# One row of the output weights moved to 32 partitions and six DMA engines, and the residual copied on chip, in a decode layer of attention and gated FFN

## The chip, the cores and the metric

The kernel runs on one core of one Trainium2 chip. The time is device microseconds of one execution. The profile is a record of one execution; its span, the time from first to last recorded instruction, is about 1.7 us shorter than the device time. Every execution also reports its span (to 0.1 us) and its mean granted TensorE clock, so spans can be compared even where only one execution has a full trace.

## The reference, cut to what matters

```python
xn = layernorm(A_x)                                  # 8 tokens, D = 512
# attention: 32 query heads, 8 kv heads, the last 1024 cached positions
q = xn @ wq
o = softmax(q @ k.T * Dh**-0.5) @ v
s = o.reshape(8, 4096) @ wo                          # wo is 4096 x 512, 4 MB
g = silu((gelu(xn @ w_gate) * (xn @ w_up)) @ w_down)
return A_x + s * g
```

Everything is bf16 and every weight and cache byte is used once. The 47.5 MB that must come in from memory set the pace: the packets of queue q1, 47.46 MB, take 95.0% of the span of the 16 DMA engines.

## The kernel before: the parts that matter

`wo` is loaded as 128 partitions of 32 rows each, in shrinking pieces so that little is left to compute after the last one lands. Two tiny loads bring the residual x into the layout of the result.

```python
NOR = Hq * Dh // P                                        # 32
wo_rows = A_wo.rearrange("(p j) d -> p (j d)", j=NOR)
# ...
        if g == NGR:
            parts = [(0, 16), (16, 24), (24, 28), (28, 30), (30, 31), (31, 32)]
            wo_t = [load_wo(*q) for q in parts[:2]]
            for t in range(2):
                nc.sync.dma_start(
                    out=x_res[64 * t : 64 * t + B, :], in_=x_flat[:, t * 256 : (t + 1) * 256]
                )
            wo_t += [load_wo(*q) for q in parts[2:]]
# ... score, soft, values of the last groups; then the FFN
    hT = ffn_up()            # contains regroup(), which makes og, the attention output by row
    ffn_down(hT)
    nc.vector.tensor_copy(out=x_b, in_=x_res)
    s_ps = ps_big.tile([P, 512], FP32, name="big")
    for q, (j0, j1) in enumerate(parts):
        for j in range(j0, j1):
            for t in range(2):
                c0 = (j - j0) * D + t * 256
                nc.tensor.matmul(
                    s_ps[64 * t : 64 * t + 64, 0:256],
                    og[:, j : j + 2, :].rearrange("p m b -> p (m b)"),
                    wo_t[q][:, c0 : c0 + 256],
                    start=(j == 0), stop=(j == NOR - 1),
                    tile_position=(0, 64 * t), skip_group_check=True,
                )
    nc.vector.tensor_tensor(out=tmp, in0=s_ps[:, 0:256], in1=g_sb, op=ALU.mult)
    nc.vector.tensor_tensor(out=out_sb, in0=tmp, in1=x_b, op=ALU.add)
    # ... two output DMAs
```

The softmax here doesn't subtract the row's maximum and nothing guards it: scores larger than these inputs give would overflow.

Of the kernel before, what the change touches and what calls it, by code (L numbers as in the profile page):

```python
# [9 lines left out]
ALU = mybir.AluOpType  # L10
AX = mybir.AxisListType
BF16 = mybir.dt.bfloat16
FP32 = mybir.dt.float32
# [3 lines left out]
def kernel(  # L17
# [13 lines left out]
    nc = tc.nc  # L31

    B, Sq, D = A_x.shape
# [11 lines left out]
    P = nc.NUM_PARTITIONS  # L45
# [12 lines left out]
    consts = ctx.enter_context(tc.tile_pool(name="consts", bufs=1))  # L58
    wide = ctx.enter_context(tc.tile_pool(name="wide", bufs=NWIDE))
    ring = ctx.enter_context(tc.tile_pool(name="ring", bufs=NSLOT))  # L60
    persist = ctx.enter_context(tc.tile_pool(name="persist", bufs=1))
# [8 lines left out]
    ps_a = ctx.enter_context(tc.tile_pool(name="ps_a", bufs=1, space=bass.MemoryType.PSUM))  # L70
# [5 lines left out]
    def slot():  # L76
        return ring.tile([P, SLOT], BF16, name="slot", align_bytes=512)
# [4 lines left out]
    x_flat = A_x.flatten_outer_dims()  # L82
    x_sb = persist.tile([B, D], BF16, name="x_sb")
    x_res = persist.tile([P, D // 2], BF16, name="x_res")
    nc.gpsimd.memset(x_res, 0.0)



    wq_rows = A_wq.rearrange("(p k) n -> p (k n)", k=NDC)

# [8 lines left out]
    def load_kv(cache, b, i):  # L99
        t = slot()  # L100
        nc.sync.dma_start(
            out=t,
            in_=cache[b, i * HN : (i + 1) * HN, win0:Sk, :].rearrange(
                "n (p r) d -> p n (r d)", r=NKR
            ),
        )
        return t

    def load_up(w):
        return load_wide(w.rearrange("(p k) n -> p (k n)", k=NDC), 0, NDC * F)  # L110

    def load_down():
        return load_wide(B_w_down.rearrange("(p j) d -> p (j d)", j=FR), 0, FR * D)

    NOR = Hq * Dh // P
    wo_rows = A_wo.rearrange("(p j) d -> p (j d)", j=NOR)

    def load_wo(j0, j1):

        if (j1 - j0) * D > SLOT:  # L120
            return load_wide(wo_rows, j0 * D, j1 * D)
        t = slot()
        nc.sync.dma_start(out=t[:, 0 : (j1 - j0) * D], in_=wo_rows[:, j0 * D : j1 * D])
        return t

    groups = [(b, i) for i in range(NHALF) for b in range(B)]
    NGR = len(groups)
    k_t, v_t = {}, {}
# [16 lines left out]
        out=ident,  # L145
        in_=ident,
# [6 lines left out]
    perm = consts.tile([P, P], BF16, name="perm")  # L153
    nc.gpsimd.tensor_copy(
        out=perm.rearrange("p (h q) -> p h q", q=P // 32),
        in_=ident.rearrange("p (q h) -> p h q", q=P // 32),
    )
    ident_f = consts.tile([P, P], FP32, name="ident_f")
    nc.vector.tensor_copy(out=ident_f, in_=ident)
    ones_f = consts.tile([P, P], FP32, name="ones_f")  # L160
# [5 lines left out]
        out=hot.rearrange("n r (m j) -> n r m j", m=HN),  # L166
        in_=hot.rearrange("n r (m j) -> n r m j", m=HN),
# [9 lines left out]
        out=far.rearrange("n (c m) -> n c m", m=HN),  # L177
        in_=far.rearrange("n (c m) -> n c m", m=HN),
# [9 lines left out]
        out=selq,  # L188
        in_=ident.rearrange("p (m q) -> p q m", q=QW),
        axis=AX.X,  # L190
        op=ALU.add,
# [3 lines left out]
        out=selr.rearrange("p r q -> p (r q)"),  # L195
        in_=ident.rearrange("p (u c) -> p c u", u=4),
        axis=AX.X,
        op=ALU.add,
# [12 lines left out]
        out=xhat[0:B, :],  # L211
        in0=x_sb,
# [19 lines left out]
    oT_all = persist.tile([P, B, Hq], BF16, name="oT_all")  # L232
    og = persist.tile([P, NOR + 1, 32], BF16, name="og")
    nc.vector.memset(og, 0.0)

    kT_t, p_t, pT_t, ss_t, o_t = {}, {}, {}, {}, {}

# [16 lines left out]
    def score(g):  # L254

        b, i = groups[g]
        sc = ps_sc.tile([P, 512], FP32, name="sc_ps")
        sc_t[g] = sc
        kT = kT_t[g].rearrange("w (r k e) -> w r k e", k=P, e=2)
        nc.tensor.matmul(  # L260
            sc,
            hot.rearrange("n r q -> n (r q)"),
            far,
            start=True,
            stop=False,
            skip_group_check=True,
        )
        for e in range(2):
            for t in range(4):
                nc.tensor.matmul(  # L270
                    sc[32 * t : 32 * t + 32, :],
                    q2_all[:, i, b, e, :, :, :].rearrange("w r n j -> w (r n j)"),
                    kT[:, :, 32 * t : 32 * t + 32, e],
                    start=False,
                    stop=(e == 1),
                    skip_group_check=True,
                    tile_position=(0, 32 * t),
                )

    def soft(g):  # L280
        p = p_pool.tile([P, 512], BF16, name="p")
        acc = small.tile([P, 1], FP32, name="acc")
        nc.scalar.activation(  # L283
            out=p, in_=sc_t[g], func=ACT.Exp, scale=inv_sqrt_dh, accum_out=acc
        )
        p_t[g] = p, acc

    def turn_p(g):
        p, acc = p_t[g]
        pT = pT_pool.tile([P, 512], BF16, name="pT")  # L290
        nc.vector.transpose(out=pT, in_=p)  # L291
        pT_t[g] = pT
        ss = small.tile([P, QW], FP32, name="ss")
        nc.vector.tensor_scalar(
            out=ss, in0=selq, scalar1=acc[:, 0:1], scalar2=None, op0=ALU.mult
        )
        ss_t[g] = ss
# [43 lines left out]
    def regroup():  # L341

        zt = ffn_sb.tile([P, B * Hq], BF16, name="zt")
        nc.vector.transpose(out=zt, in_=oT_all.rearrange("p b h -> p (b h)"))
        rg = ps_a.tile([P, B, 32], FP32, name="rg_ps", tag="a")
        nc.tensor.matmul(
            rg.rearrange("p b j -> p (b j)"),
            perm,
            zt,
            start=True,  # L350
            stop=True,
        )
        nc.vector.tensor_copy(
            out=og[:, 0:NOR, 0:B], in_=rg.rearrange("p b j -> p j b")
        )


    for t in range(4):
# [3 lines left out]
    for k in range(NDC):  # L362
        for i in range(NHALF):
            for j in range(HN):
# [5 lines left out]
                    start=(k == 0),  # L370
                    stop=(k == NDC - 1),
                    tile_position=(0, 32 * j),
                    skip_group_check=True,
                )
    q_sb = persist.tile([P, NHALF, rep, 2, 2, Dh // 2], BF16, name="q_sb")
    for i in range(NHALF):
        for rr in range(2):
            copy = nc.scalar.copy if rr else nc.vector.tensor_copy
            copy(  # L379
                out=q_sb[:, i, :, :, rr, :],  # L380
                in_=q_ps[i].rearrange("p (j w e) -> p j e w", j=rep, e=2),
            )
    for i in range(NHALF):
# [8 lines left out]
        for e in range(2):  # L392
            for rr in range(2):
                copy = nc.scalar.copy if rr else nc.vector.tensor_copy
                copy(  # L395
                    out=q2_all[64 * rr : 64 * rr + 64, i, :, e, rr, :, :].rearrange(
                        "p b n j -> p j n b"
                    ),
                    in_=qT_ps[64 * rr : 64 * rr + 64, :, e, :, 0:B],
# [41 lines left out]
        )  # L441
        return hT

    x_b = persist.tile([P, D // 2], BF16, name="x_b")
    g_sb = persist.tile([P, D // 2], FP32, name="g_sb")
    nc.vector.memset(g_sb, 0.0)

# [29 lines left out]
    for g in range(NGR + 1):  # L477
        if g < NGR:
            v_t[g] = load_kv(A_v_cache, *groups[g])
            if g + 2 < NGR:  # L480
                k_t[g + 2] = load_kv(A_k_cache, *groups[g + 2])
        if g == NGR - 1:
            wg_t = load_up(B_w_gate)
            wu_t = load_up(B_w_up)
            wd_t = load_down()
        if g == NGR:

            parts = [(0, 16), (16, 24), (24, 28), (28, 30), (30, 31), (31, 32)]
            wo_t = [load_wo(*q) for q in parts[:2]]
            for t in range(2):  # L490
                nc.sync.dma_start(
                    out=x_res[64 * t : 64 * t + B, :], in_=x_flat[:, t * 256 : (t + 1) * 256]
                )
            wo_t += [load_wo(*q) for q in parts[2:]]
        if g < NGR:
            score(g)
            soft(g)
        if g + 1 < NGR:
            turn_k(g + 1, 0)
        if g < NGR:  # L500
            turn_p(g)
        if g + 1 < NGR:
            turn_k(g + 1, 1)
        if g:
            values(g - 1)
        if g + 1 < NGR:
            turn_k(g + 1, 2)
            turn_k(g + 1, 3)
        if g:
            gather(g - 1)  # L510
# [1 line left out]
    hT = ffn_up()  # L512
    ffn_down(hT)

    nc.vector.tensor_copy(out=x_b, in_=x_res)


    s_ps = ps_big.tile([P, 512], FP32, name="big")
    for q, (j0, j1) in enumerate(parts):
        for j in range(j0, j1):  # L520
            for t in range(2):
                c0 = (j - j0) * D + t * 256
                nc.tensor.matmul(  # L523
                    s_ps[64 * t : 64 * t + 64, 0:256],
                    og[:, j : j + 2, :].rearrange("p m b -> p (m b)"),
                    wo_t[q][:, c0 : c0 + 256],
                    start=(j == 0),
                    stop=(j == NOR - 1),
                    tile_position=(0, 64 * t),
                    skip_group_check=True,  # L530
                )
    tmp = ffn_sb.tile([P, 256], BF16, name="tmp")
    out_sb = ffn_sb.tile([P, 256], BF16, name="out_sb")
    nc.vector.tensor_tensor(out=tmp, in0=s_ps[:, 0:256], in1=g_sb, op=ALU.mult)
    nc.vector.tensor_tensor(out=out_sb, in0=tmp, in1=x_b, op=ALU.add)
    out_flat = out.flatten_outer_dims()
    nc.sync.dma_start(out=out_flat[:, 0:256], in_=out_sb[0:B, :])
    nc.scalar.dma_start(out=out_flat[:, 256:512], in_=out_sb[64 : 64 + B, :])
# [30 lines left out]
```

## Time and profile before

| | before |
|---|---|
| time, median (6 runs) | 120.83 us (120.77 to 120.98) |
| span of the profiled run | 119.1 us |
| data moved by queue q1 | 47.46 MB |
| last landing of the last `wo` load | 115.60 us |
| end of the last matmul, start of `tmp` | 115.96, 115.98 us |

Lines of the page of before: the span, the busy time by engine, the clock and DMA rows (40 slices of the span, tenths), and two of the DMA queues.

```profile
span 119.1 us, 2281 instructions
PE 86.8 (73%) x929; PEld 62.1 (52%) x929; DVE 64.2 (54%) x149; ACT 40.4 (34%) x78; POOL 4.2 (4%) x10
...
PEclk9999999555799999999999999999999965555999
DMA  4999999999999999999999999999999999999940
...
q1 hardware_dynamic: 6240, 47.46, 95.0%
q8 instruction: 7, 0.11, 0.3%
```

The DMA row is 9 from slice 1 to slice 37 and the chain of waits is 57% DMA, so DMA bounds the kernel. The DMA row ends with a 4 and a 0: not every engine is busy to the end. Queue q8 is no data of the kernel: seven packets of instructions, 16 KB each.

The end of the chain of waits of before (start us, length us, what):

```profile
100.62 13.72 DMA slot<-in_A_wo_dram
114.34 0.04 issue
114.38 0.63 PE big L523 x8
115.01 0.00 issue
115.02 0.63 PE big L523 x6
...
115.98 0.44 DVE tmp L534
```

The windows view of before (a one-microsecond stretch; busy time and count of each engine; then granted clock, DMA share, GB/s):

```profile
109.00:110.00 1.00, 0.00 (x0) 0.00 (x0) 0.46 (x2) 0.37 (x1) 0.00 (x0) 0.71 0.90 377
...
111.00:112.00 1.00, 1.00 (x24) 1.00 (x20) 0.41 (x1) 0.00 (x0) 0.00 (x0) 1.00 1.02 419
...
114.00:115.00 1.00, 0.79 (x12) 0.43 (x8) 0.00 (x0) 0.00 (x0) 0.00 (x0) 1.00 0.50 181
115.00:116.00 1.00, 0.94 (x9) 0.43 (x7) 0.02 (x1) 0.00 (x0) 0.00 (x0) 1.00 0.06 22
```

The DMA share falls to a half between 114 and 115 us and to 0.06 in the microsecond after.

The trace file also records each landing, though no view of the profile lists them: a load's semaphore is raised several times, 16 times for a `wo` load on 128 partitions and 8 times for an `x_res` load on 8. Each increment is taken here as the landing of one DMA engine; that is the author's reading, as the trace numbers no engines. All landings below are read from there. For the last load of before (row 31, 16 engines, times in us):

```
113.90 113.95 114.00 114.07 114.08 114.13 | 114.32 114.58 114.85 | 115.24 115.29 115.37 115.39 115.53 115.58 115.60
```

Six engines are done 1.1 to 1.7 us before the seven late ones, though an even share of the load's 128 packets of 1 KB is eight for each (an estimate: packets divided by increments). The change tries to use that.

### The profile page before, as it was taken

Reading aid. Unit: us, or ns where it says so; the run is one execution under the profiler, and the core shown is the slowest. Engines: PE = TensorE matmul, PEld = TensorE weight load, DVE = VectorE, ACT = ScalarE, POOL = GpSimd, SP = SyncE. Lnnn points to the kernel's source line nnn. Section 1 sums busy time; section 2 is a strip of 40 time slices with the busy share of each in tenths; the row PEclk is TensorE's granted clock in tenths of the full one; section 3 lists DMA queues with packets and bytes.
Section 4 is the critical chain, followed back from the end, with each engine's and each line's share of the span. In section 5 each row is a group of like instructions: output and inputs, shape, how many; then the busy total and the mean of one; then the engine's idle time right before and its main releaser. Section 6 shows DMA issues by size and latency. Waiting matters only on the chain.

```text
span 119.1 us, 2281 instructions
## 1 busy us (share of the span) xinstructions
PE 86.8 (73%) x929; PEld 62.1 (52%) x929; DVE 64.2 (54%) x149; ACT 40.4 (34%) x78; POOL 4.2 (4%) x10
## 2 busy tenths in 40 slices
PE   0013946786999999999998797977979843546680
PEld 0003813563767777686775584755847630133650
DVE  5340644643666866876694664945748424622211
ACT  4000314792443562464354342453424403001100
POOL 7600000000000000000000000000000000000000
PEclk9999999555799999999999999999999965555999
DMA  4999999999999999999999999999999999999940
GB/s 88 432 396 440 418 426 432 418 432 424 418 432 432 432 402 435 429 418 426 429 426 421 429 424 421 429 426 424 429 424 442 426 424 448 420 440 402 405 165 3
DMA packets 6281, 47.61 MB, mean 400 GB/s; under 512 B 728, under 2 KB 1024, under 8 KB 1280
## 3 DMA queue, kind: packets, MB, share of 16 engines
q1 hardware_dynamic: 6240, 47.46, 95.0%
q8 instruction: 7, 0.11, 0.3%
q10 hardware_dynamic: 32, 0.01, 0.0%
q14 instruction: 2, 0.02, 0.0%
HBM read 47.46 MB, written 0.01 MB: 399 GB/s over the span
## 4 chain that ended last, share of the span: by engine, by line
DMA 57%; PE 24%; DVE 10%; ACT 2%; SPq 2%; issue 1%; DVEq 0%
DMA wide_slot<-in_B_w_gate_dram 18%; DMA slot<-in_A_v_cache_dram 16%; PE t_ps L244 12%; DMA slot<-in_A_wo_dram 12%; DMA wide_slot<-in_A_wq_dram 11%; DVE kT L250 8%; PE sc_ps L270 5%; PE o_ps L304 3%; PE big L411 1%; PE big L523 1%; DVE q_all L395 1%; ACT q_all L395 1%; PE big L366 1%; DVE q_sb L379 1%; ACT p L283 1%
## 5 line engine op out<-in xcount | busy, mean ns | idle before, releaser
L250 DVE COPY kT<-t_ps 128x1024 bf16<-128x1024 bf16 x48 | 31.8, 688 | 26.4 <-PE t_ps L244 24.5
L244 PE MATMUL t_ps<-ident_f,slot 128*128 128x128 f32 x256 | 38.5, 301 | 7.8 <-DMA slot<-in_A_k_cache_dram 7.8
L244 PEld LDWEIGHTS t_ps<-ident_f,slot 128*128 128x128 f32 x256 | 31.2, 154 | 18.0 <-issue 7.2
L250 ACT COPY kT<-t_ps 128x1024 bf16<-128x1024 bf16 x16 | 16.2, 1012 | 16.9 <-PE t_ps L244 16.5
L283 ACT ACTIVATE p<-sc_ps 128x512 bf16<-128x512 f32 x16 | 9.6, 597 | 28.4 <-PE sc_ps L270 28.4
L270 PE MATMUL sc_ps<-kT,q_all 128*32 128x512 bf16 x128 | 10.7, 405 | 3.9 <-ACT q_all L395 1.8
L291 DVE STREAM_TRANSPOSE pT<-p 128x512 bf16<-128x512 bf16 x16 | 11.2, 703 | 2.8 <-ACT p L283 2.8
L304 PE MATMUL o_ps<-slot,pT 128*32 128x256 bf16 x256 | 10.1, 278 | 0.0
L324 PE MATMUL a_ps<-selr,o_sb 128*128 128x16 f32 x64 | 9.6, 263 | 0.4 <-ACT o_sb L314 0.3
L324 PEld LDWEIGHTS a_ps<-selr,o_sb 128*128 128x128 f32 x64 | 8.4, 192 | 0.6 <-ACT o_sb L314 0.6
L270 PEld LDWEIGHTS <-q_all 128*32 128x32 bf16 x128 | 3.3, 95 | 7.9 <-issue 3.2
L304 PEld LDWEIGHTS <-pT 128*32 128x32 bf16 x256 | 5.5, 97 | 2.9 <-issue 2.5
L314 ACT COPY o_sb<-o_ps 128x256 f32<-128x256 f32 x16 | 6.0, 378 | 1.3 <-PE o_ps L304 1.3
L260 PE MATMUL sc_ps<-far,hot 4*128 4x512 bf16 x16 | 6.4, 398 | 0.0
L411 PE MATMUL big<-wide_slot,xT 128*32 128x448 bf16 x32 | 3.4, 571 | 3.8 <-DMA wide_slot<-in_B_w_up_dram 2.2
L523 PEld LDWEIGHTS <-og 128*64 128x64 bf16 x64 | 3.5, 109 | 3.7 <-DMA wide_slot<-in_A_wo_dram 2.1
L220 PE MATMUL t_ps<-ident,xhat 32*128 32x32 bf16 x4 | 0.3, 195 | 6.6 <-DVE xhat L210 6.6
L320 PEld LDWEIGHTS a_ps<-ss,ones_f 128*128 128x128 f32 x32 | 4.8, 191 | 0.5 <-DVE oT_all L334 0.3
L453 PE MATMUL big<-wide_slot,hT 128*32 128x256 bf16 x28 | 3.2, 417 | 2.6 <-DMA wide_slot<-in_B_w_down_dram 2.6
L320 PE MATMUL a_ps<-ss,ones_f 128*128 128x16 f32 x32 | 4.9, 229 | 0.0
L333 DVE RECIPROCAL rs<-a_ps 128x16 f32<-128x16 f32 x16 | 4.0, 249 | 1.3 <-PE a_ps L324 1.2
L453 PEld LDWEIGHTS <-hT 128*32 128x32 bf16 x28 | 2.2, 142 | 3.9 <-DVE hT L438 3.4
(64 smaller groups left out, 50.5 us busy)
## 6 DMA issues: line engine op xcount, KB each, us to landing
slot<-in_A_k_cache_dram SPq DMA_DIRECT2D x16, 1024.0 KB, 19.7
slot<-in_A_v_cache_dram SPq DMA_DIRECT2D x16, 1024.0 KB, 19.8
wide_slot<-in_A_wq_dram SPq DMA_DIRECT2D x2, 2048.0 KB, 13.7
wide_slot<-in_A_wo_dram SPq DMA_DIRECT2D x1, 2048.0 KB
wide_slot<-in_B_w_gate_dram SPq DMA_DIRECT2D x1, 1792.0 KB, 21.4
wide_slot<-in_B_w_up_dram SPq DMA_DIRECT2D x1, 1792.0 KB, 23.2
wide_slot<-in_B_w_down_dram SPq DMA_DIRECT2D x1, 1792.0 KB, 25.0
slot<-in_A_wo_dram SPq DMA_DIRECT2D x1, 1024.0 KB
```

The lines of the kernel that those rows point to most:

```text
L244: nc.tensor.transpose(kp[:, c * P : (c + 1) * P], kw[:, rp * P : (rp + 1) * P], ident_f)
L250: copy(out=kT_t[g][:, t * 8 * P : (t + 1) * 8 * P], in_=kp.bitcast(BF16))
L260: nc.tensor.matmul(sc, hot.rearrange("n r q -> n (r q)"), far, start=True, stop=False, skip_group_check=True,)
L270: nc.tensor.matmul(sc[32 * t : 32 * t + 32, :], q2_all[:, i, b, e, :, :, :].rearrange("w r n j -> w (r n j)"), kT[:, :, 32 * t : 32 * t + ...
L283: nc.scalar.activation(out=p, in_=sc_t[g], func=ACT.Exp, scale=inv_sqrt_dh, accum_out=acc)
L291: nc.vector.transpose(out=pT, in_=p)
L304: nc.tensor.matmul(o_ps[32 * u : 32 * u + 32, :], pT_t[g][:, m * 32 : (m + 1) * 32], v_t[g][:, m * 256 : (m + 1) * 256], start=(m < 4), st ...
L314: nc.scalar.copy(out=o_sb, in_=o_ps)
L320: nc.tensor.matmul(a_ps[:, 0, :], ones_f, ss_t[g], start=True, stop=True, skip_group_check=True)
L324: nc.tensor.matmul(a_ps[:, 1, :], o_t[g][:, r * Dh : (r + 1) * Dh], selr[:, r, :], start=(r == 0), stop=(r == 1), skip_group_check=True,)
L453: nc.tensor.matmul(f_ps[64 * t : 64 * t + 32, 0:256], hT[:, j, :], wd_t[:, c0 : c0 + 256], start=(j == 0), stop=(j == FR - 1), tile_positi ...
L523: nc.tensor.matmul(s_ps[64 * t : 64 * t + 64, 0:256], og[:, j : j + 2, :].rearrange("p m b -> p (m b)"), wo_t[q][:, c0 : c0 + 256], start= ...
```

## The change

Intent: take the last row of each partition (row 31) away from the late engines. Of its 128 pieces of 1 KB, 126 go out with an outer dimension of 6, so that six DMA engines carry 21 packets each and the others none; the attention output is regrouped to match by five small matmuls with a selection matrix. The piece is multiplied third, so its engines have time. The residual is copied on chip from the x that is there already.

```diff
+    NX, XR = 24, 5
+    def load_last():
+        last = A_wo.rearrange("(p j) d -> p j d", j=NOR)[:, NOR - 1, :]
+        six = last[0:126, :].rearrange("(e m) d -> e m d", m=21)
+        wx = slot()
+        nc.sync.dma_start(out=wx[0:NX, 0 : XR * D], in_=six[:, 0:20, :])
+        nc.sync.dma_start(out=wx[NX : NX + 6, 0:D], in_=six[:, 20, :])
+        nc.sync.dma_start(out=wx[NX + 6 : 32, 0:D], in_=last[126:128, :])
+        return wx
 ... selx, a 128 x 5 x 32 selection matrix, made by POOL from perm; in regroup():
+        rx = ps_a.tile([32, XR, B], FP32, name="rx_ps", tag="a")
+        for r in range(XR):
+            nc.tensor.matmul(rx[:, r, :], selx[:, r, :], zt...[:, :, NOR - 1], ...)
+        nc.vector.tensor_copy(out=ox[:, 0:XR, 0:B], in_=rx)
 ...
-            parts = [(0, 16), (16, 24), (24, 28), (28, 30), (30, 31), (31, 32)]
+            parts = [(0, 16), (16, 24), (24, 28), (28, 30), (30, 31)]
             wo_t = [load_wo(*q) for q in parts[:2]]
-            ... two loads of x_res
+            wx = load_last()
             wo_t += [load_wo(*q) for q in parts[2:]]
 ...
-    nc.vector.tensor_copy(out=x_b, in_=x_res)
+    for t in range(2):
+        nc.gpsimd.tensor_copy(out=x_res[64 * t : 64 * t + B, :], in_=x_sb[:, t * 256 : (t + 1) * 256])
 ...
     for q, (j0, j1) in enumerate(parts):
+        if q == 2:
+            for r in range(XR):
+                project(ox, wx, r, r * D, NX if r else 32)     # 2 matmuls each
         for j in range(j0, j1):
             project(og, wo_t[q], j, (j - j0) * D)
```

More of the change, by code (lines that the diff above doesn't have):

```diff
@@ L157 @@
     )
+    selx = consts.tile([P, XR, 32], BF16, name="selx")
+    nc.gpsimd.memset(selx, 0.0)
+    six = perm[:, 0:126].rearrange("p (e m) -> p e m", m=21)
+    for r in range(XR):
+        nc.gpsimd.tensor_copy(
+            out=selx[:, r, 0:NX].rearrange("p (e i) -> p e i", i=4),
+            in_=six[:, :, r:20:XR],
+        )
+    nc.gpsimd.tensor_copy(out=selx[:, 0, NX : NX + 6], in_=six[:, :, 20])
+    nc.gpsimd.tensor_copy(out=selx[:, 0, NX + 6 : 32], in_=perm[:, 126:128])
     ident_f = consts.tile([P, P], FP32, name="ident_f")
@@ L234 @@
     nc.vector.memset(og, 0.0)
+    ox = persist.tile([32, XR + 1, 32], BF16, name="ox")
+    nc.gpsimd.memset(ox, 0.0)
     kT_t, p_t, pT_t, ss_t, o_t = {}, {}, {}, {}, {}
@@ L355, in regroup @@
         )
+        rx = ps_a.tile([32, XR, B], FP32, name="rx_ps", tag="a")
+        for r in range(XR):
+            nc.tensor.matmul(
+                rx[:, r, :],
+                selx[:, r, :],
+                zt.rearrange("p (b j) -> p b j", b=B)[:, :, NOR - 1],
+                start=True,
+                stop=True,
+                skip_group_check=True,
+            )
+        nc.vector.tensor_copy(out=ox[:, 0:XR, 0:B], in_=rx)
     for t in range(4):
@@ L442, in ffn_up @@
         return hT
-    x_b = persist.tile([P, D // 2], BF16, name="x_b")
     g_sb = persist.tile([P, D // 2], FP32, name="g_sb")
@@ L486 @@
         if g == NGR:
-            parts = [(0, 16), (16, 24), (24, 28), (28, 30), (30, 31), (31, 32)]
+            parts = [(0, 16), (16, 24), (24, 28), (28, 30), (30, 31)]
             wo_t = [load_wo(*q) for q in parts[:2]]
-            for t in range(2):
-                nc.sync.dma_start(
-                    out=x_res[64 * t : 64 * t + B, :], in_=x_flat[:, t * 256 : (t + 1) * 256]
-                )
+            wx = load_last()
             wo_t += [load_wo(*q) for q in parts[2:]]
@@ L513, with project @@
     ffn_down(hT)
-    nc.vector.tensor_copy(out=x_b, in_=x_res)
+    for t in range(2):
+        nc.gpsimd.tensor_copy(
+            out=x_res[64 * t : 64 * t + B, :], in_=x_sb[:, t * 256 : (t + 1) * 256]
+        )
     s_ps = ps_big.tile([P, 512], FP32, name="big")
+    def project(o, w, j, c0, n=P):
+        for t in range(2):
+            nc.tensor.matmul(
+                s_ps[64 * t : 64 * t + 64, 0:256],
+                o[0:n, j : j + 2, :].rearrange("p m b -> p (m b)"),
+                w[0:n, c0 + t * 256 : c0 + (t + 1) * 256],
+                start=(j == 0 and o is og),
+                stop=(j == NOR - 2 and o is og),
+                tile_position=(0, 64 * t),
+                skip_group_check=True,
+            )
     for q, (j0, j1) in enumerate(parts):
+        if q == 2:
+            for r in range(XR):
+                project(ox, wx, r, r * D, NX if r else 32)
         for j in range(j0, j1):
-            for t in range(2):
-                c0 = (j - j0) * D + t * 256
-                nc.tensor.matmul(
-                    s_ps[64 * t : 64 * t + 64, 0:256],
-                    og[:, j : j + 2, :].rearrange("p m b -> p (m b)"),
-                    wo_t[q][:, c0 : c0 + 256],
-                    start=(j == 0),
-                    stop=(j == NOR - 1),
-                    tile_position=(0, 64 * t),
-                    skip_group_check=True,
-                )
+            project(og, wo_t[q], j, (j - j0) * D)
     tmp = ffn_sb.tile([P, 256], BF16, name="tmp")
@@ L534 @@
     nc.vector.tensor_tensor(out=tmp, in0=s_ps[:, 0:256], in1=g_sb, op=ALU.mult)
-    nc.vector.tensor_tensor(out=out_sb, in0=tmp, in1=x_b, op=ALU.add)
+    nc.vector.tensor_tensor(out=out_sb, in0=tmp, in1=x_res, op=ALU.add)
     out_flat = out.flatten_outer_dims()
```

## The prediction

Engine 0, 1, 2, ... are names, here and in all that follows: 0 and 1 are the engines of a load on two partitions, and each further number is the engine that a load on one partition more adds. That the six engines of the change are 0 to 5, and those of the x_res loads 0 to 7, was an assumption. The sum came to 114.85 - 0.39 + 0.85 = 115.31 us for the last landing, so 0.30 us off 120.83, or 120.53 us. In it, 0.33 us (8 packets) and 0.06 us (x_res) were estimates from the landings of before, and 0.85 us is 21 packets at about 0.04 us.

> **What bounds the kernel.** DMA. The page's DMA row is 9 in every slice from 1 to 37, at 400 to 448 GB/s; the chain of waits gives DMA 57%. In the windows view the DMA share stays 0.94 or more from 95 to 113 us, then falls to 0.91, 0.50 and 0.06 in the next three microseconds. So the sixteen DMA engines do not finish together. The trace's landing records show it: the sixteen increments of the last wo load (row 31) come at 113.90 to 114.13 us (six), 114.32, 114.58, 114.85, then 115.24 to 115.60 (seven). The page's part 3 lists seven 16 KB instruction packets (0.9 to 1.0 us each in the trace); landings that were within 0.6 us at 20 us fall apart after such packets, one engine at a time. I take the seven late engines to be the seven hit by them.
>
> After the last landing comes a serial tail: two matmuls (timeline: 115.64, 0.31 us), tmp 0.44, out_sb 0.29, output issue and landing, to 119.1.
>
> **What the change does.** Row 31 costs every engine 8 packets of 1 KB: the landings of the last two loads differ by 0.29 to 0.34 us on each engine, about 0.038 us per packet. The two x_res loads (512 B packets) cost eight engines about 0.06 us. Both leave the late engines. In their place 126 of the 128 rows go out with outer dimension 6. [...] the x_res loads on 8 partitions landed in 8 increments, the wo loads in 16. So engines 0 to 5 get 21 packets (two of them 22), about 0.85 us, in place of 0.33 + 0.06.
>
> Are 0 to 5 the early ones? The x_res landings (engines 0 to 7) come at 111.47, 111.52, 111.63, 111.71, 112.14, 112.39, 112.93, 113.27: six early or middling, two late. I believe that the six are 0 to 5. The slowest of them ended at 114.85; it should now end at 114.85 - 0.39 + 0.85 = 115.31. Late engines end at 115.30. A balance: last landing 115.3 in place of 115.6.
>
> PE: ten matmuls of wx take the place of two. Issue interval is about 0.053 us (8 in 0.63, 16 in 1.06), so ten cost 0.53. They stand after rows 16 to 23 (issued by 113.97), when wx is in (about 113.1), and end near 114.5; rows 24 to 27 land at about 114.34, so PE is 0.15 late there, catches up before rows 28 and 29 (115.0), and waits for row 30 at 115.3. Last matmul ends near 115.65, was 115.96.
>
> Off the critical path: about 2.5 us of POOL work near 2 us (q2_all ready near 7 us, needed at 18.6); five small matmuls and a copy after regroup (PE waits for w_up until 101.5 anyway); x copied on POOL early; x_b copy dropped.
>
> **Predicted:** 120.83 - 0.30 = 120.53 us; 8 in 10: 120.30 to 120.90. Faster by over 2%: 0.005; within: 0.985; slower by over 2%: 0.01.
>
> **Would show it right:** first wx load landing in 6 increments, row 30 landing last near 115.3 with its sixteen increments closer together, tmp starting 0.3 us earlier, PE idle before row 30. **Wrong:** PE the releaser without a DMA wait, or an early half that stays early.
>
> **What could break it:** engines 0 to 5 include a late one (then about 0.5 us slower), instruction packets falling on other engines or at other times, 1 KB reads at a 32 KB pitch slower on six engines.

## More of the kernel before

The clock row shows two stretches at half speed; the second one ends three to four slices from the end.

TensorE has its full clock from 109.6 us on, just before the projection, and follows the loads.

All executions here were classed as fast, except one of the version called `five`, which was slow and is left out, and the single unclassified executions of the two probes.

Ratios below are the mean time of one kernel's fast runs over that of the other's of the same rounds, so not quite the ratio of the medians that are quoted.

## The result, and the profile after

The changed kernel took 121.59 us (median of 6 runs, 121.32 to 121.96), before 120.83 in the same rounds: ratio 1.0064, 95% interval 1.0046 to 1.0081. It is 0.76 us slower, where 0.30 us faster was forecast (120.30 to 120.90 us, eight times in ten).

Lines of the page after that answer to those of before:

```profile
span 120.2 us, 2317 instructions
PE 89.6 (74%) x942; PEld 64.0 (53%) x942; DVE 64.0 (53%) x149; ACT 40.5 (34%) x78; POOL 6.5 (5%) x21
...
PEclk9999999855599999999999999999999975555587
DMA  4999999999999999999999999999999999999910
```

The end of its chain of waits:

```profile
98.21 12.27 DMA wide_slot<-in_A_wo_dram
110.48 0.04 issue
110.53 6.57 PE big L557 x69
117.09 0.02 issue
117.12 0.44 DVE tmp L575
```

Its windows view:

```profile
109.00:110.00 1.00, 0.00 (x0) 0.00 (x0) 0.59 (x2) 0.27 (x1) 0.00 (x0) 0.50 0.90 377
...
111.00:112.00 1.00, 1.00 (x12) 0.84 (x10) 0.28 (x1) 0.00 (x0) 0.00 (x0) 0.50 1.05 422
...
114.00:115.00 1.00, 1.00 (x12) 0.83 (x10) 0.00 (x0) 0.00 (x0) 0.00 (x0) 0.50 0.48 176
115.00:116.00 1.00, 1.00 (x20) 0.71 (x14) 0.00 (x0) 0.00 (x0) 0.00 (x0) 0.98 0.03 10
```

Two things differ. First, the whole projection is one stretch of 6.57 us in which PE waits for nothing: its clock stayed at a half until 115.05 us, so it did 12 matmuls in a microsecond where before did 24, and it ended 1.1 us later than before's. Second, the landings. Of the first wx load (six engines), and of the last load (row 30, sixteen):

```
wx:      112.08 112.17 112.23 112.68 113.06 113.62
row 30:  113.57 113.67 113.74 113.79 | 114.34 114.50 114.51 114.80 114.87 115.03 115.05 115.09 115.10 115.14 | 115.34 115.84
```

One of the six engines lands its share 1.5 us behind the first, and ends the whole load at 115.84 us, 0.24 us after before's last landing. The engines that carry no wx end at 115.14 at the latest, by the spacing of the landings (wx to row 30 is 2.2 us on the latest engine, so 113.06 belongs to 115.34 and 113.62 to 115.84). So two theories stand:

- A, imbalance: one of engines 0 to 5 is a late one, and the 21 packets lengthen the latest path.
- B, clock: in this execution PE, with eight more matmuls in the projection and half a clock, finished last.

The slowdown is not a fluke of the profiled execution: the other five were also slower, 121.32 to 121.73 us, at a mean clock of 0.9, the same as before's. That mean does not decide between A and B, since it does not say where in the span the half clock fell: the profiled executions of onerow_five and extra_pe below also have 0.9, with half clock until 114.3 and 114.2 us, where before's ended at 109.6.

### The profile page after: what moved, and what is told of

Read it like the earlier page. It is cut to its first block, busy times and chain, and to the rows that moved or that the text cites. A ratio compares the mean times of both kernels' runs of the same rounds, so it can differ in the third digit from the quotient of the medians.

```text
span 120.2 us, 2317 instructions
## 1 busy us (share of the span) xinstructions
PE 89.6 (74%) x942; PEld 64.0 (53%) x942; DVE 64.0 (53%) x149; ACT 40.5 (34%) x78; POOL 6.5 (5%) x21
## 4 chain that ended last, share of the span: by engine, by line
DMA 52%; PE 30%; DVE 10%; ACT 4%; issue 1%; SPq 0%; DVEq 0%
DMA wide_slot<-in_B_w_gate_dram 18%; DMA slot<-in_A_v_cache_dram 16%; PE t_ps L269 13%; DMA wide_slot<-in_A_wo_dram 10%; DMA slot<-in_A_k_cache_dram 8%; DVE kT L275 6%; PE big L557 5%; PE sc_ps L295 4%; PE o_ps L329 3%; ACT q_all L431 2%; PE big L402 2%; DVE q_all L431 2%; ACT L308 1%; PE big L447 1%; DVE q_sb L415 1%
## 5 line engine op out<-in xcount | busy, mean ns | idle before, releaser
L269 PE MATMUL t_ps<-ident_f,slot 128*128 128x128 f32 x256 | 39.0, 302 | 6.8 <-DMA slot<-in_A_k_cache_dram 6.5
L557 PEld LDWEIGHTS <-og 128*64 128x64 bf16 x62 | 4.7, 156 | 3.1 <-DMA wide_slot<-in_A_wo_dram 2.1
L447 PE MATMUL big<-wide_slot,xT 128*32 128x448 bf16 x32 | 2.7, 467 | 3.7 <-DMA wide_slot<-in_B_w_up_dram 2.1
L557 PE MATMUL big<-wide_slot,og 128*64 128x256 bf16 x32 | 3.6, 421 | 1.7 <-DMA wide_slot<-in_A_wo_dram 1.7
```

Source lines behind the costliest of these rows:

```text
L269: nc.tensor.transpose(kp[:, c * P : (c + 1) * P], kw[:, rp * P : (rp + 1) * P], ident_f)
L557: nc.tensor.matmul(s_ps[64 * t : 64 * t + 64, 0:256], o[0:n, j : j + 2, :].rearrange("p m b -> p (m b)"), w[0:n, c0 + t * 256 : c0 + (t + ...
```

## The experiments

Each was run beside executions of before on the same chip (together they are one job); the table collects them. "Filling" means extra matmuls on unused data that keep TensorE's clock up (mean clock 0.943 to 0.971 in the executions of warm_before, 0.886 to 0.927 in those of before beside them). "Span" is the median over the executions, "over before" its distance to before's median span of the same job. "Last landing" is from the one execution with a trace.

| version | DMA engines for row 31 | filling | ratio of times [95%] | span (over before) | last landing |
|---|---|---|---|---|---|
| after2 | 6 | no | 1.0037 [1.0015, 1.0058] | 119.6 (+0.3) | 115.82 |
| onerow | 6 | no | 1.0042 [1.0011, 1.0072] | 119.6 (+0.3) | 116.07 |
| wx16 | 16, on 16 partitions | no | 1.0113 [1.0078, 1.0148] | 120.3 (+1.0) | 116.70 |
| xonly | 16, as before | no | 1.0022 [0.9997, 1.0046] | 119.2 (-0.1) | 115.64 |
| warm_before | 16, as before | yes | 0.9996 [0.9983, 1.0009] | 119.0 (0.0) | 115.43 |
| warm_after | 6 | yes | 1.0060 [1.0042, 1.0077] | 119.45 (+0.45) | 116.16 |
| warm_five | 5 | yes | 1.0020 [0.9993, 1.0048] | 119.1 (0.0) | 115.60 |
| five | 5 | no | 1.0035 [1.0007, 1.0062] | 119.6 (+0.5) | 115.57 |
| warm_mix | 5, and 16 | yes | 1.0040 [1.0010, 1.0070] | 119.1 (0.0) | 115.62 |
| fetch9 | 16, as before | no | 1.0025 [0.9989, 1.0061] | 119.3 (+0.2) | 115.61 |
| extra_pe | 16, as before | no | 1.0010 [0.9989, 1.0032] | 119.35 (+0.25) | 115.56 |
| onerow_five | 5 | no | 1.0037 [1.0002, 1.0072] | 119.45 (+0.35) | 115.61 |

### The changed kernel again: after2

No edit; a second profile.

> The changed kernel once more, for a second profile. Theory A (imbalance: one of the DMA engines 0 to 5 is a late one, and gets 21 packets more): 121.3 to 121.7 us, the last load lands 0.2 to 0.3 us later than before's 115.60 in every profile, and PE waits for it. Theory B (clock: the half-speed stretch of TensorE, which ended at 109.6 us before and at 115.1 in the first profile after, covers the output projection): the time follows the clock; a profile whose half-speed stretch ends by about 111 us shows a time near 121.0, PE waiting for DMA. Both can be true; then A is worth 0.25 and B the rest.

121.29 us median (121.20 to 122.54). The profiled execution was the slowest, 122.54 us: half clock until 116.4 us, PE busy for 7.23 us without a wait, in its chain of waits:

```profile
110.42 7.23 PE big L557 x72
117.65 0.02 issue
```

Yet the last landing was again late, 115.82, and again one of the six wx landings stood out (112.17, 112.23, 112.23, 112.81, 113.18, 113.56). Both theories stay open. Note the size: in this second job the same kernel is 0.37% slower than before (0.3 us in the median span), where the first job had 0.64%.

The trace file also records when the granted clock changes. In before it is halved from 20.83 to 31.07 us (10.24 us) and from 95.93 to 109.58 us (13.65); in the profile after from 22.89 to 33.13 (10.24) and from 97.98 to 115.05 (17.07). From one length to the next it is 3.41 and 3.42 us, and they are three, four and five times that; in both traces the second stretch begins 75.1 us after the first, 22 times that. So in these two traces the half clock begins and ends on the steps of a grid (an estimate from these lengths), and the grid's phase differs between the two executions.

### As many matmuls as before: onerow

```diff
-            for r in range(XR):
+            for r in range(1):
                 project(ox, wx, r, r * D, NX if r else 32)
```

> Wrong result on purpose: the wx loads stay, but only one of their five rows is multiplied, so PE has as many matmuls in the projection as before (64). A: the last landing stays late, time within 0.1 us of the changed kernel where PE waited for DMA. B: the eight matmuls are on the path, time falls by 0.4 (full clock, 8 x 0.053) to 0.85 us (half clock, 8 x 0.107).

(0.053 us is worked out from before at full clock, 8 matmuls in 0.63 us and 16 in 1.06; 0.107 is twice that, an estimate. For 32 matmuls before has 1.94 us at full clock and the profile after 3.62 us at half.)

Its output is wrong, which doesn't matter for the time. 121.33 us, no faster than the changed kernel (121.29 us in the same rounds), as A expected and B did not. The last landing was 116.07 us. Fewer matmuls alone do not bring the time back. The trace by itself does not separate the two: the half clock lasted to 114.6 us here, and the last two matmuls start at 116.14 us, just after the last landing.

### All sixteen engines, on 16 partitions: wx16

```diff
-    NX, XR = 24, 5
+    NX, XR = 16, 8
-        ... the three loads
+        nc.sync.dma_start(out=wx[0:NX, 0 : XR * D], in_=last.rearrange("(e m) d -> e m d", m=XR))
```

> The last row on 16 partitions, 8 rows each, outer dimension 16: all 16 engines get 8 packets again, as before the change, but it is loaded third; 16 matmuls in place of 10. A: the last landing returns to about 115.6 us, time 120.8 to 120.9 although PE has 14 more matmuls than before. B: slower than the changed kernel by 0.3 (full clock) to 0.65 us (half clock), 121.8 or more.

122.17 us. The number fits B's expectation, but not for B's reason: in its profile the clock was full from 109.4 us and PE waited for the loads. The timeline of wx16 (start us, length us, engine, line, what; in brackets the idle time before it and what ended it):

```profile
110.62 1.94 PE L550 MATMUL big<-wide_slot,og 128*64 128x256 bf16 x32 [1.67 <-DMA wide_slot<-in_A_wo_dram]
113.97 1.06 PE L550 MATMUL big<-slot,og 128*64 128x256 bf16 x16 [1.41 <-DMA slot<-in_A_wo_dram]
114.96 1.06 PE L550 MATMUL big<-slot,ox 16*64 16x256 bf16 x16
115.95 1.48 PE L550 MATMUL big<-slot,og 128*64 128x256 bf16 x14
```

Rows 16 to 23 landed at 113.92 at the latest (before: 113.07) and the last load at 116.70, 1.1 us after before's, with the same 128 pieces spread over sixteen engines. So the experiment brought a new cost and does not decide between A and B. What the cost comes from, the sixteen partitions, the row pitch or the 16 matmuls, is not shown: no run here took them apart.

### The residual alone: xonly

```diff
-            ... two loads of x_res
-    nc.vector.tensor_copy(out=x_b, in_=x_res)
+    for t in range(2):
+        nc.gpsimd.tensor_copy(out=x_res[64 * t : 64 * t + B, :], in_=x_sb[:, t * 256 : (t + 1) * 256])
```

> Before with only the residual copied on chip. Both theories: within 0.1 us of before, 120.75 to 120.85; the two small loads cost eight engines 0.06 us each.

121.07 us, ratio 1.0022 with an interval that just includes 1. The spans are before's (119.2, before 119.3); the 0.06 us per engine, an estimate from the landings of before, is too small for these runs to show. What is more lies outside the span: time less span is 1.80 to 1.94 us, for before 1.62 to 1.73. That part is not settled; see warm_five below. In the profiled execution the half clock lasted to 115.3 us and PE was the last to finish, 5.95 us without a wait although the last load had landed at 115.64 us, as before's:

```profile
110.66 5.95 PE big L521 x64
116.61 0.02 issue
```

So this fate is not the change's alone: kernels with before's matmul count can meet it too.

### Which engines are late: probe_lo and probe_hi

The trace does not number DMA engines. By its increments it shows on how many a load lands (8 for x_res on 8 partitions, 16 for `wo` on 128). The author assumed that a load on k partitions lands on the same engines as one on k - 1 and on one more. If so, loads on k = 2, 3, 4, ... partitions reveal the engines one by one, and the one that k adds is called engine k - 1.

```diff
-            parts = [(0, 16), (16, 24), (24, 28), (28, 30), (30, 31), (31, 32)]
+            parts = [(0, 16), (16, 32)]
+            probe = slot()
+            for i, k in enumerate((2, 3, 4, 5, 6, 7)):        # probe_hi: 9, 10, 11, 12, 13, 14
+                nc.sync.dma_start(out=probe[0:k, i * 256 : (i + 1) * 256], in_=A_wo[0:k, 0:256])
```

> Not a version to time: before with the residual copied on chip, rows 16 to 31 of wo in one load, and six 512-byte-row loads on 2, 3, 4, 5, 6 and 7 partitions behind it. Each lands in as many increments as it has partitions; what the load on k partitions shows more than the one on k-1 is the lateness of engine k-1. Theory A (one of engines 0 to 5 is a late one): exactly one of engines 0 to 5 lands over 1 us behind the earliest, two about 0.3 and 0.7 us behind. Against A: all six land within 0.8 us.

> The same with loads on 9 to 14 partitions, to place the other late engines. A: six more late ones (over 1 us behind) among engines 6 to 15, so that no choice of the six lowest avoids all.

Each load, on 2 to 7 and on 9 to 14 partitions, landed in as many increments as it has partitions. Every landing of one probe is found again about 0.18 us later in the next (k=2 to k=3: 113.88 to 114.06, 114.54 to 114.72), and the one that is left over is the new engine. Landings of probe_lo (the new one in brackets):

```
k=2:  113.88  114.54
k=3:  [113.94]  114.06  114.72
k=4:  114.11  114.23  [114.78]  114.89
k=5:  [113.90]  114.29  114.42  114.97  115.07
k=6:  114.09  114.47  114.60  115.16  115.24  [115.47]
k=7:  114.28  114.65  114.78  115.34  115.42  [115.46]  115.67
```

Less 0.18 us for the probe, the load before them ended at 113.7 us on the early engines and at 115.2 to 115.4 on the late ones. Engines 2 and 4 are early, one of 0 and 1 is early and the other 0.7 us behind, engine 3 about 0.9 behind; engine 5 is late, and so is engine 6. In probe_hi the new landings are 113.98 for engine 9, early, and 115.23, 115.36, 115.43 and 115.53 for engines 10 to 13, late. The nine landings for k=9 hold five early, two middling and two late ones, so 7 and 8 are early if the first seven are among them, and one of 14 and 15 must be the seventh late one if there are seven as in before.

A is right as to the engines: 5 is late. That the wx loads of the changed kernel go to 0 to 5 is still read from their landings alone, and these fit: the first lands in six increments, three early, two middling and one late (112.08 to 113.62 us in the profile after), and with an outer dimension of 5 (warm_five below) in five, three early and two middling. The x_res landings of before (four early, two middling, two late among engines 0 to 7) fit the same set; the two late ones were then 5 and 6, not 6 and 7.

### The clock taken out: warm_before and warm_after

```diff
+    def keep_busy(n):                       # matmuls on unused data into the free score bank
+        fill = ps_sc.tile([P, 512], FP32, name="sc_ps")
+        for _ in range(n):
+            nc.tensor.matmul(fill, ident, kT_t[NGR - 1][:, 0:512], start=True, stop=True, skip_group_check=True)
     regroup()
+    keep_busy(10)
     ...
+    keep_busy(6)
     hT = ffn_up()
+    keep_busy(13)
     ffn_down(hT)
+    keep_busy(12)
```

> Before with 41 matmuls on unused data in the gaps of TensorE between 95 and 110.6 us, so that its clock is never halved there. Theory B (the half clock makes PE the last to finish in some executions): one state of times, 120.6 to 120.85 us, with less spread than before has; profile without a half-speed stretch after 92 us, PE waiting for each wo load from rows 16 on.

> The changed kernel with the same 41 matmuls. A: slower than warm_before by 0.25 to 0.5 us, as its last landing is later by that much, although the clock is full in both. If B alone were the cause: equal to warm_before or 0.3 us faster, as predicted.

warm_before: 120.67 us (120.62 to 120.69), before in the same rounds 120.66 (120.57 to 121.09). The median is unchanged and the spread is gone. warm_after: 121.39 us (121.22 to 121.81), 0.72 us above warm_before. Both have the full clock from 34 us to 118 us (the windows of warm_after from 113 to 117 us: 1.00). The timeline of warm_before:

```profile
110.46 1.94 PE L537 MATMUL big<-wide_slot,og 128*64 128x256 bf16 x32 [0.46 <-DMA wide_slot<-in_A_wo_dram]
112.94 1.06 PE L537 MATMUL big<-slot,og 128*64 128x256 bf16 x16 [0.55 <-DMA slot<-in_A_wo_dram]
114.18 1.59 PE L537 MATMUL big<-slot,og 128*64 128x256 bf16 x16 [0.17 <-DMA slot<-in_A_wo_dram]
```

and of warm_after:

```profile
110.70 1.94 PE L571 MATMUL big<-wide_slot,og 128*64 128x256 bf16 x32 [0.45 <-DMA wide_slot<-in_A_wo_dram]
113.15 1.06 PE L571 MATMUL big<-slot,og 128*64 128x256 bf16 x16 [0.51 <-DMA slot<-in_A_wo_dram]
114.18 0.73 PE L571 MATMUL big<-slot,ox 32*64 32x256 bf16 x10
115.23 1.28 PE L571 MATMUL big<-slot,og 128*64 128x256 bf16 x14 [0.31 <-DMA slot<-in_A_wo_dram]
```

PE now runs as the prediction assumed: 32 matmuls in 1.94 us, ten of wx in 0.73 us, then it waits for rows 24 to 27, and at the end for row 30 (the line for 14 matmuls hides that wait): the last two matmuls start at 116.21 us, 0.05 us after the last landing, in warm_before at 115.47 us, 0.04 us after it. The loads are late: the last landing is 116.16 us against 115.43, 0.73 us, and the spans differ by 0.7 us in these two profiled executions (119.7 and 119.0), by 0.45 us in the median. So A costs by itself, with the clock full. Of the 0.72 us in device time, about 0.27 us is no part of the span: time less span is 1.82 to 2.31 us for warm_after and 1.62 to 1.69 us for warm_before. That part is open, as for xonly.

### Engine 5 left out: warm_five and five

```diff
-    NX, XR = 24, 5
+    NX, XR = 20, 6
-        six = last[0:126, :].rearrange("(e m) d -> e m d", m=21)
+        six = last[0:125, :].rearrange("(e m) d -> e m d", m=25)
-        nc.sync.dma_start(out=wx[0:NX, 0 : XR * D], in_=six[:, 0:20, :])
-        nc.sync.dma_start(out=wx[NX : NX + 6, 0:D], in_=six[:, 20, :])
-        nc.sync.dma_start(out=wx[NX + 6 : 32, 0:D], in_=last[126:128, :])
+        nc.sync.dma_start(out=wx[0:NX, 0 : XR * D], in_=six[:, 0:24, :])
+        nc.sync.dma_start(out=wx[NX : NX + 5, 0:D], in_=six[:, 24, :])
+        nc.sync.dma_start(out=wx[NX + 5 : NX + 8, 0:D], in_=last[125:128, :])
 ... selx to match; warm_five also has keep_busy as above
```

> warm_after with outer dimension 5 in place of 6: engines 0 to 4 take 25 packets each (were 21), engine 5, the late one in the probe, none; 12 matmuls of wx in place of 10. Theory A (engine 5 is late and its 21 packets came last): the late landing at 116.1 is gone; the slower of the two middling engines, at 115.3 with 21 packets, ends near 115.5; 120.7 to 120.8 us, as warm_before, 0.6 under warm_after. Rival C (1 KB packets at a wide pitch on few engines are slow in themselves, or the extra PE work costs): as slow as warm_after or slower, since both grow.

> The same without the filling matmuls, so to be compared with the changed kernel itself. A: 120.8 to 121.1 us, 0.3 to 0.5 under the changed kernel, with some executions up to 0.9 above where the half clock covers the projection. C: 121.3 or more.

The landings did what A said. Of warm_five:

```
wx:      112.22 112.35 112.37 112.90 113.32
row 30:  113.44 113.52 113.66 113.76 114.53 114.63 114.71 114.94 115.03 115.14 115.16 115.17 115.19 115.20 115.24 115.60
```

No landing of wx stands out, and the last landing is 115.60 us (expected 115.5), though each engine carries more than with six. Theory C, that few engines with many small packets are slow in themselves, falls: it expected warm_five to be as slow as warm_after. The spans of warm_five's six executions are 119.0 to 119.3 us; their median is before's of the same job, where warm_after's was 0.45 us over. There is no gain over before either: the last engine is now the middling one with 25 packets.

The device times did not follow as cleanly, and both missed A's expectation: warm_five 121.04 us (120.77 to 121.84, expected at most 120.8), five 121.28 us in its fast executions (120.83 to 121.89, expected at most 121.1). For five the spans are long too (119.1 to 120.2, median 119.6). For warm_five they are not. So leaving engine 5 out brings the span back with the clock kept full, but without filling it does not: five is 0.35% over before, the changed kernel in after2 0.37%.

### Split by lateness: warm_mix

```diff
+        nc.sync.dma_start(out=wx[0:20, 0 : 4 * D], in_=last[0:80, :].rearrange("(m e) d -> e m d", e=5))
+        nc.sync.dma_start(out=wx[20:68, 0:D], in_=last[80:128, :])
 ... selx, ox to match; keep_busy
```

> Row 31 split by lateness: 80 of its 128 rows on engines 0 to 4 (16 packets each), 48 on all sixteen (3 each, were 8). A: late engines end at 115.14 + 3 x 0.04 = 115.26, the middling one at 115.34 - 2 x 0.04 = 115.26, in place of warm_before's 115.43: 120.5 us, 0.15 to 0.2 under warm_before. C: 120.7 or more.

A miss. The last landing was 115.62 us, not 115.26. The load of three packets per engine took the late engines 0.2 to 0.3 us (rows 16 to 23 landed on them at 112.94 to 113.31, this load at 113.16 to 113.60), not 0.12. Whether that is a cost of the load itself or of its partitions (20 to 67) was not tried. This was the attempt to beat both kernels, and it does not.

### What makes an engine late: fetch9

The landings of before come apart in steps. At 20 us the sixteen engines are within 0.6 us. A load that lands after the first instruction packet (28.0 us) has one engine a full 1.0 us behind the next (33.82 and 32.79). After six packets, the w_gate load has six late engines (96.86 to 97.23 us, the early ones 95.46 to 95.69). After the seventh (109.3 us), rows 16 to 23 have seven (112.69 to 113.07, early 111.29 to 111.56). Counted as the engines over 1.2 us behind the earliest, the loads after the first to the seventh packet (first landings at 32.28, 51.90, 66.62, 76.43, 86.24, 95.46 and 111.29 us) have 1, 2, 3, 4, 5, 6 and 7 late engines, and each packet takes 0.88 to 1.04 us. Before has seven such packets, and 929 matmuls and 929 weight loads: about 265 instructions to a packet if these are what the packets carry (an estimate from the page of before). If serving such a packet is what makes a DMA engine late, more TensorE instructions make more late engines. The edit adds 160 matmuls and their weight loads, 320 instructions, before 7 us (in before the first matmul starts at 6.64 us).

```diff
+    spin = ps_o.tile([P, 2 * Dh], FP32, name="o_ps")
+    for _ in range(160):                  # before 7 us, where TensorE is idle
+        nc.tensor.matmul(spin[:, 0:32], ident, ident[:, 0:32], start=True, stop=True, skip_group_check=True)
```

> Before with 160 small matmuls on unused data before 7 us, where TensorE is idle: 320 instructions more[...]. If a DMA engine is late because it served an instruction packet: 8 or 9 instruction packets and 8 or 9 landings over 1 us behind the earliest at the end, in place of 7, the early group smaller by as many; the last landing and the time about as before. If lateness has another cause: still seven late ones.

There are eight instruction packets (7.1, 23.3, 41.0, 51.8, 64.0, 76.8, 87.7 and 101.1 us), and rows 16 to 23 have eight late landings (112.84 to 113.13 us), two middling ones and six early ones (111.25 to 111.49). The last landing, 115.61 us, is before's. So the count follows the instruction packets, in before step by step and here with one more. What makes an engine middling is not explained. Which engine gets which packet was seen only as the final set in the probes.

### The spread of warm_five: warm_five_b, warm_five_c, warm_five_d, warm_before_b

No edit; further profiles, to learn why device times of warm_five spread while warm_before's do not.

> warm_five again for one more profile. If the set of late engines changes (D): an execution at 121.2 us or more shows one of the five wx increments over 1 us behind the earliest, and a last landing of 115.9 or later; one at 120.8 shows none. If the clock does it (B): the last landing is 115.6 in every profile, and in a slow one PE has no wait before the last rows.

> As warm_five_b, another profile: D: a slow execution has one of the five wx increments over 1 us behind the earliest and a last landing of 115.9 us or later. B: last landing at 115.6 us always.

> As warm_five_b, another profile: D: a slow execution has one of the five wx increments over 1 us behind the earliest and a last landing of 115.9 us or later. B: last landing at 115.6 us always.

> warm_before again: last landing 115.4 to 115.6 us and 120.6 to 120.8 us, whichever engines are late, since all sixteen take equal shares and the latest alone counts.

Neither theory as put was right. The last landings were 115.65, 115.54 and 115.68 us, warm_before_b's 115.64, and in none of the three did a wx landing stand out. So the set of late engines was the same each time. One execution (warm_five_c, span 119.7) had a half clock from 94.0 to 100.8 us, in which the filling matmuls themselves made PE late. But the main spread lies outside the span: time less span was 1.66 to 2.84 us over warm_five's first six executions, for warm_before 1.62 to 1.69. In two traces where it was large (2.22 us in warm_five_b, 2.62 us in warm_mix) one more 16 KB instruction packet starts after the span, at 120.4 and 121.0 us, and takes 1.3 and 1.1 us. That accounts for those two executions at best; xonly's 0.2 us has no such packet in its trace. For the changed kernel it is small, 1.70 to 1.76 us against before's 1.6 to 1.7 us.

### The matmuls alone, and both causes taken away: extra_pe and onerow_five

```diff
+        if q == 2:                        # extra_pe: before with eight more matmuls, into an unused bank
+            fill = ps_sc.tile([P, 512], FP32, name="sc_ps")
+            for r in range(8):
+                t = r % 2
+                nc.tensor.matmul(fill[64 * t : 64 * t + 64, 0:256], og[:, r : r + 2, :]..., wo_t[1][:, t * 256 : (t + 1) * 256], ...)
```

onerow_five is `five` with `range(1)` as in onerow.

> Before with eight more matmuls of the projection's shape, on data that lies ready and into an unused bank, at the place where the changed kernel has those of wx; no DMA changed, no filling. If the matmuls are a second cause: spans 0.2 to 0.45 us over before's in most executions (8 x 0.053 at full, 8 x 0.107 at half clock, less the wait of PE that they fill), last landing unchanged at 115.4 to 115.6. If not: within 0.1 us of before.

> Wrong result on purpose: outer dimension 5, but only one of the six rows of wx is multiplied, so PE has the 64 matmuls of before. Both causes taken away without filling matmuls: spans as before's, within 0.1 us, where five had 0.4 more and onerow 0.45 more. If something else in the change costs: 0.3 or more over before.

extra_pe: last landing 115.56 us, spans 119.1 to 119.7, median 119.35, before 119.1; ratio 1.0010 with an interval from 0.9989 to 1.0032. The direction is as expected and the size is within the noise: not shown. onerow_five missed its expectation: median span 119.45 us, 0.35 over before, although both its landings (last 115.61) and its matmul count are before's. Its trace shows the clock at a half until 114.3 us:

```profile
110.58 3.63 PE L557 MATMUL big<-wide_slot,og 128*64 128x256 bf16 x32 [1.69 <-DMA wide_slot<-in_A_wo_dram]
114.00 1.21 PE L557 MATMUL big<-slot,og 128*64 128x256 bf16 x16
115.13 0.30 PE L557 MATMUL big<-slot,ox 28*64 28x256 bf16 x2
115.36 0.96 PE L557 MATMUL big<-slot,og 128*64 128x256 bf16 x14
```

So B is real in single executions, and it can fall on a kernel with before's matmul count. In the traces without filling the half clock ended at 114.2 to 116.4 us in after, after2, onerow, onerow_five, xonly and extra_pe, and at 109.1 to 109.6 us in before, five, fetch9 and wx16. With one or two traces of each it is not shown that the changed kernel meets it oftener than before does. One hint of what decides is in the traces: before and after2 have the same phase (half clock from 95.93 and 95.92 us), and before's clock rises at 109.58 us while after2's does not. In the last 3.41 us before that rise, 106.2 to 109.6 us, PE is busy with before's w_down matmuls (105.83 to 109.0) for 2.83 us, and in after2, whose last ended at 108.7, for about 2.6 us. That PE's busy time in such a step decides is the author's guess. Two executions do not make a threshold, and all 20 traces together show none: the least PE busy time in such a step at whose end the clock rose is 2.83 us, the most at whose end it did not is 3.19 us (warm_five_c).

## Why the prediction was wrong

- "A balance: last landing 115.3 in place of 115.6" failed, and the step that failed is "I believe that the six are 0 to 5". The x_res landings showed six engines of eight not late; the probe shows that they were 0 to 4 and 7, with 5 and 6 late. Engine 5 got 21 packets though it was the latest of the six (115.47 us in the probe on 6 partitions, where the earliest landed at 114.09). The prediction's own sum for a late engine, 115.60 - 0.39 + 0.85 us, gives 116.06 us. The last landing was 115.82 to 116.16 us in the four traces with six engines (mean 115.97), and 115.54 to 115.68 in the six traces with five engines.
- The price of that mistake was rightly foreseen as a risk ("engines 0 to 5 include a late one (then about 0.5 us slower)"), though the forecast, "8 in 10: 120.30 to 120.90", left little room for it. With the clock full, warm_after's median span is 0.45 us over before's, and warm_five's 0.0. Without filling that gain did not appear (five).
- "About 0.85 us" for 21 packets was about right: the first wx load, 20 of the 21, landed at 112.08 us, 0.85 after rows 16 to 23 on the earliest engine (111.23), and in row 30 the first engine with wx (114.34) is 0.77 us behind the first without (113.57). So was 115.31 us for the slowest middling engine: next to the late one, the latest landing in the four traces with six engines is 115.27 to 115.46. With five engines and 25 packets each this middling engine is the last, at 115.54 to 115.68 us, and so even five engines gain nothing.
- "PE ... waits for row 30 at 115.3" assumed the full clock of before's trace (0.053 us per matmul). In the first trace after, PE had half of it (32 matmuls in 3.62 us, not 1.94) and never waited. The prediction read one execution's clock as a property of the kernel. With the clock kept full (warm_after), PE waited as forecast, but for a row 30 that came at 116.16 us.
- The seven late engines "hit by" instruction packets: supported by the step-by-step count in before and by fetch9, eight packets and eight late engines.
- The residual: forecast as 0.06 us on engines that do not decide. The spans agree (119.2 against 119.3 us). About 0.2 us outside the span in xonly was not foreseen and is not explained.
- How the 0.76 us adds up is only shown in part: at full clock the imbalance costs 0.45 us of span. The changed kernel without filling was 0.3 us of span over before in after2, so the rest of the first job's 0.76 us did not return there, and leaving engine 5 out (five) did not lower the time there either. The split between imbalance, half clock, added matmuls and chance is open for the kernel without filling.

No version here beats before. warm_before has its median and a smaller spread in one job (120.62 to 120.69 us).

## What to carry to other kernels

Here the last two matmuls start only after the latest landing of the last load (warm_after: 116.21 us, 0.05 us after it; warm_before: 115.47 us, 0.04 us after it), so a load that is confined to few engines must be confined to the right ones. At full clock, six engines of which one was late cost 0.45 us of span, and five without it 0.0. Find out which are late by loads on 2, 3, 4, ... partitions before building on a guess, and count the bytes that the slowest chosen engine can still take. A list of landings without engine numbers tells how many are late, not which. Where the tail of a kernel relies on TensorE keeping up, look at the clock in several traces, since one is not like the next: in the two traces of the changed kernel the half clock ended at 115.05 and at 116.4 us, and with before's matmul count it ended at 109.6 us (before), 114.3 (onerow_five) and 115.3 (xonly).
